# One expert's rows fetched by index instead of gathered by matrix products, and the index search moved from chunk 6 to chunk 2

## The chip, the cores and the metric

The kernel runs on 1 core of one Trainium2 chip. The metric is the device time of one execution in microseconds (us). TensorE is called PE here, VectorE DVE, ScalarE ACT, GpSimd POOL and SyncE SP. PE has two clock levels, 1.2 and 2.4 GHz, and the profile gives the granted share of the full one.

## What is computed

Three layers follow each other: attention with a top-32 mask, a soft mixture of 8 experts over 32 slots, and a noisy top-2 mixture of 8 experts. The change lies in the last one, whose reference is:

```python
def _moe2_ref(x, w_gate, w_noise, noise, w1, w2):      # N=2304 D=512 E=8 F=1024
    logits = x @ w_gate
    noise_scale = np.log1p(np.exp(x @ w_noise))
    noisy_logits = logits + noise_scale * noise
    top2 = np.argpartition(-noisy_logits, 2, axis=1)[:, :2]
    ...
    for e in range(E):
        for k in range(2):
            mask = top2[:, k] == e
            h = np.maximum(x[mask] @ w1[e], 0.0)
            out[mask] += top2_w[mask, k, None] * (h @ w2[e])
    return out
```

The second layer's output is a product of a [2304, 32] matrix of weights (`cn` in the kernel) and 32 slot outputs (`soT`). `top2_w` is the softmax over the two chosen logits. So the kernel never forms x in the third layer: a token is its row of 32 weights, and an expert's first layer is applied to the 32 slot outputs once (`soT` times w1[e], 32 x 1024) and then mixed per token.

## The kernel before

**Stages.** `attention` fills some 480 us of the span, `moe` computes the second layer, the gate and what the first expert needs, and `gated` runs the eight experts of the third layer from about 511 us on.

**An expert** takes up to CAP = 640 tokens in JT = 5 row groups of 128. `CTS[e]` (128 x 640) holds the 32 weights of each of its tokens in split form, transposed; `GSS[e]` holds `soT` times w1[e], split in a high and a low half (`gh`, `gl`) and stacked by `stacked_g` with four DMAs. Its hidden width of 1024 goes in 8 chunks of 128 columns; the loop variable n counts the 64 chunks of all experts, e = n // 8, c = n % 8. Chunk n consists of

- `split(n + 2)` (L1284): the weights w2[e] of a later chunk are split in `wh` (copy, on ACT for expert 0, else on DVE) and `wl` (DVE subtraction, L1292);
- `second(n, ...)` (L1294): 5 row groups of 3 products each (L1300 to L1302) into the accumulators `ACC`;
- `first(n + 2)` (L1268), between row groups 1 and 2: two products (L1276) into the PSUM tile `hp`, then `hh` = relu on ACT (L1281) and `hl` = the remainder on DVE (L1282). `hp` is one buffer, so `first(n + 3)` waits for `hl` of n + 2.

After chunk 7 `store(e)` (L1304) copies the accumulators and POOL adds them to the output rows of the expert's tokens by five indirect DMAs (L1312), whose row numbers `ids_of(e)` takes from the fetched rows.

**How an expert gets its tokens.** Experts 0 and 1 (ED = 2) have one-hot matrices: for each of 18 blocks of tokens `slot1` gives the place of each token, DVE or ACT builds a one-hot tile, and PE multiplies it with the weighted rows `xw`. For expert 0 that is `compact` (L1138), ahead of the chunks. For expert 1 it is `hot` (L1210) and `piece` (L1223), 34 products (L1229) in chunks 1, 2, 4 and 5 as the table `PIECES` says. At the pieces named in `WT1` the first layer of expert 2 (half a = 0) or 3 (a = 1) is computed beside them by `weigh1` (L936 to L940), two products side by side in PE's columns, and `pieces_end` (L1238) splits it into `gh`, `gl`.

Experts 2 to 7 are fetched: `addresses` (L1081, seven small DVE operations in chunk 0) computes the place of every (token, choice); `spread` (L1091) gives the steps that turn places into a list of rows: `far` (POOL) with `near` (ACT), or `same` (DVE), build one-hot tiles over the position, `columns` (two DVE and four POOL operations) one-hot tiles over the column, and `rows_of_slots` (L1122, chunk 6) multiplies them in 36 small products (L1125); five DVE operations make `ridx` of it. `rows(e)` (L1242) is five indirect DMAs of POOL that fetch the rows from `XD`, `slots(e)` (L1252) three DVE operations that split them, `turn` (L1261) five transposes by PE (L1264) and the copies to `CTS[e]`. In this version chunk 7 issues `rows(2)` and `rows(0)` (the latter for `ids_of(0)`), chunk 9 `rows(1)`; from then on `rows(e + 1)` is issued in chunk c = 1, `slots(e + 1)` follows in c = 3 and `turn` in c = 4 and 5.

**Order.** Each engine works through its own instructions in the order in which the code emits them; waits are by semaphore, and an instruction that waits holds back all behind it on its engine. SP issues the weight loads in the order of the list `order`; `MORE` (L174) says after which chunks one more load is issued, and a load waits until the buffer it overwrites has been read (`used`). First-layer weights of experts 4 to 7 are used by `first_weights` (L957) after chunks 18 and 19, four products side by side.

```python
1348                weighted(1, t2.tile([128, TT, NS], F32, name="xw", bufs=1), V)
1349                addresses()
1350                pairs, far, near, same, columns = spread(t2)
1351                for k in range(3):
1352                    far(k)
1353            if n in (1, 3, 6):
1354                near((1, 3, 6).index(n))
1355            if n == 3:
1356                columns()
1357                same(3)
1358                same(4)
```

Of the kernel before, what the change touches and what calls it, by code (L numbers as in the profile page):

```python
# [25 lines left out]
E, F, DM = 8, 1024, 512  # L26
NS = 32
NTOK = NB * S
TT = 18
CAP = 640  # L30
JT = CAP // 128
ROW = 36
ED = 2
ONACT = (2, 6, 10, 14)
NCH = 7
KW = S + 64
# [3 lines left out]
def moe_after_topk_attention(ctx: ExitStack, tc: tile.TileContext, q, k, v, phi, w1, w2, wg, wn, noise, u1, u2, qk, vt, out):  # L40
    nc = tc.nc
    V, A, G, T = nc.vector, nc.scalar, nc.gpsimd, nc.tensor

    def pool(name, bufs=1, stack=ctx, **kw):
        return stack.enter_context(tc.tile_pool(name=name, bufs=bufs, **kw))
# [55 lines left out]
    WT, wpool, held = {}, {"wa": wa}, {}  # L101
# [37 lines left out]
    def used(m, e):  # L139
        held.pop(slot[order.index((m, e))])  # L140
# [28 lines left out]


    H1, H2 = 4, 2

    PIECES = {1: 6, 2: 12, 4: 8, 5: 8}
    MORE = (0, 2, 4, 6, 8, 9, 14, 19, 22, 26, 30, 34, 38)  # L174
    FW, WT1, ENDS = (18, 19), (11, 13, 15, 17), (3, 6)

    def make_xtr(wk, xk, ps, soon, row, warm):

# [601 lines left out]
    def moe(st, xp, xs, fast):  # L780
# [9 lines left out]
        ps = pool("ps1", 1, st, space=PSUM)  # L790
# [277 lines left out]
        def place():  # L1068
            V.tensor_tensor(pe, po, cap8.unsqueeze(1).to_broadcast([128, TT, 8]), op=OP.add)
# [85 lines left out]
        def some(n):  # L1155
            for _, t in zip(range(n), todo):
                compact(t)
# [9 lines left out]
        some(H2)  # L1167
        A.copy(tots, tot[:, :144])
        place()
        some(8)  # L1170
        nc.sync.dma_start(XD[0:2 * NTOK].rearrange("(p r) f -> p (r f)", p=128), RW.rearrange("p c t f -> p (c t f)"))
        some(TT)
# [22 lines left out]
        def done():  # L1195
            tb_st.close()
            xs.close()
        gated(st, ps, halves, tw, gather, cts0, done, first_weights, weigh1, halve1, keep_g, stacked_g, GSS, begin, later,
              weighted, nt, slot1, xw, addresses, spread, rows_of_slots, ridx)


    def gated(st, ps, halves, tw, gather, cts0, done, first_weights, weigh1, halve1, keep_g, stacked_g, GSS, begin, later,
              weighted, nt, slot1, xw, addresses, spread, rows_of_slots, ridx):
        CTS, CX, XS, IDS, HH, HL, WH, WL, ACC = ({} for _ in range(9))

        H = CAP // 2
        part = []
        pieces = iter([(a, t) for a in range(2) for t in range(2 * a, TT)])

        def hot(a, t):  # L1210

            w = min(H, 128 * t + 128 - a * H)
            o = t2.tile([128, H], F32R, name="hot", bufs=6)[:, :w]
            n = nt[:, a * H:a * H + w]
            if t % 3:
                V.tensor_scalar(o, n, slot1[:, t, 1:2], None, op0=OP.is_equal)
            else:
                z = t2.tile([128, H], F32, name="far", bufs=1)[:, :w]
                A.activation(z, n, AF.Abs, bias=slot1[:, t, 1:2], scale=-1.0)
                A.activation(o, z, AF.Relu, bias=1.0, scale=-1.0)  # L1220
            return a, t, w, o

        def piece(a, t, w, o):  # L1223

            if t == 2 * a:
                part[:] = [ps.tile([128, 512], F32, name="tp")]
                if a == 0:
                    CTS[1] = t2.tile([128, CAP], F32R, name="cts")
            T.matmul(part[0][:64, :w], xw[1][:, t].rearrange("p l s -> p (l s)"), o, start=(t == 2 * a), stop=(t == TT - 1),  # L1229
                     skip_group_check=True)  # L1230

            if t in WT1:
                weigh1(2 + a, part[0], [WT1.index(t)])
            if t == TT - 1:
                for r, f in ((0, A.copy), (64, V.tensor_copy)):
                    f(CTS[1][r:r + 64, a * H:a * H + H], part[0][:64, :H])

        def pieces_end(a):  # L1238
            halve1(2 + a, part[0])
            used(2, 2 + a)  # L1240

        def rows(e):  # L1242
            xs = XS[e] = t2.tile([128, JT, ROW], F32, name="xs", bufs=3)
# [2 lines left out]
                    ap=ridx[:, e * JT + j:e * JT + j + 1], axis=0), bounds_check=2 * NTOK, oob_is_err=False)  # L1246

        def ids_of(e):
            ii = IDS[e] = t2.tile([128, JT], I32, name="ii")
            G.tensor_copy(ii, XS[e][:, :, NS])  # L1250

        def slots(e):  # L1252
# [15 lines left out]
        def first(n):  # L1268
            e, c = divmod(n, 8)

            p = [ps.tile([128, 512], F32, name=f"acc{i}") for i in ((1, 3), (2, 4))[n]] if n < 2 else halves()
            hh = HH[n] = tw.tile([128, CAP], F32R, name="hh")
            hl = HL[n] = tl.tile([128, CAP], F32R, name="hl")
            h = CAP // 2
            for a in range(2):
                T.matmul(p[a][:, :h] if n < 2 else p[:, a, :h], GSS[e][:, c * 128:c * 128 + 128],  # L1276
                         CTS[e][:, a * h:a * h + h], start=True, stop=True)
            for a in range(2) if n < 2 else [slice(None)]:
                x = p[a][:, :h] if n < 2 else p[:, :, :h]
# [14 lines left out]
        def second(n, js):  # L1294
            e, c = divmod(n, 8)
            for j in js:
                if c == 0:
                    ACC[j] = ps.tile([128, 512], F32, name=f"acc{(0, 1, 3, 2, 4)[j]}")
                r = slice(j * 128, j * 128 + 128)
                T.matmul(ACC[j], HH[n][:, r], WH[n], start=(c == 0), stop=False)  # L1300
                T.matmul(ACC[j], HH[n][:, r], WL[n], start=False, stop=False)  # L1301
                T.matmul(ACC[j], HL[n][:, r], WH[n], start=False, stop=(c == 7))  # L1302
# [18 lines left out]
        split(0, hi=False)  # L1321
        done()
        tl, t2 = pool("tl", 4, st), pool("t2", 2, st)
        first(0)
        split(1)
        first(1)
        for n in range(8 * E):
            e, c = divmod(n, 8)
            if (e, c) == (1, 0):
                later(t2)  # L1330
            m = n + 2
            some = [x for _, x in zip(range(PIECES.get(n, 0)), pieces)]
            some[:6] = [hot(*x) for x in some[:6]]
            if m < 8 * E:
                split(m)
            if n < 8 * E - 2:
                second(n, range(2))
                if m < 8 * E:
                    first(m)
                second(n, range(2, JT))  # L1340
            elif n == 8 * E - 1:

                for j in range(JT):
                    for i in (n - 1, n):
                        second(i, [j])
            if n == 0:
                begin()
                weighted(1, t2.tile([128, TT, NS], F32, name="xw", bufs=1), V)
                addresses()
                pairs, far, near, same, columns = spread(t2)  # L1350
                for k in range(3):
                    far(k)
            if n in (1, 3, 6):
                near((1, 3, 6).index(n))
            if n == 3:
                columns()
                same(3)
                same(4)
            if n in ENDS:
                pieces_end(ENDS.index(n))  # L1360
            for x in some[:6]:
                piece(*x)
            for x in some[6:]:
                piece(*hot(*x))
            if n == 6:
                rows_of_slots(ps.tile([128, 512], F32, name="tp"), pairs)
            if n == 7:
                keep_g(0)
                assert not list(pieces)
                rows(2)  # L1370
                rows(0)
                ids_of(0)
            if n == 9:
                rows(1)
                ids_of(1)
            if m % 8 == 7:
                used(3, m // 8)
            if e + 1 < E:
                if c == 1 and e + 1 != 4:
                    stacked_g(e + 1)  # L1380
                if c == 1 and e + 1 > ED:
                    rows(e + 1)
                if c == 3 and e + 1 >= ED:
                    slots(e + 1)
                if c == 4 and e + 1 >= ED:
                    turn(e + 1, 0, 4)
                if c == 5 and e + 1 >= ED:
                    turn(e + 1, 4, JT)
            if n in FW:
                first_weights(1, FW.index(n), ps.tile([128, 512], F32, name="tp"))  # L1390
            if n in MORE:
                more(32, 1)
            if (e, c) == (3, 1):
                stacked_g(4)
            if c == 6 and e >= ED:
                ids_of(e)
            if c == 7:
                store(e)

# [136 lines left out]
```

## Time and profile before

| what | value |
|---|---|
| median of 3 runs | 824.79 us (820.87 to 827.76) |
| the profiled execution's own time | 822.0 us |
| its span (first to last instruction) | 820.2 us |
| PE busy over the span | 768.7 us (94%) |
| DVE, ACT, POOL busy | 603.1, 500.3, 488.9 us |
| mean granted PE clock | 0.968 |

The profile comes from one execution, which is 2.8 us below the median. The page cuts the span in 40 slices of 20.5 us; its lines of the busy share (tenths) and of the granted clock are:

```profile
PE   8999999999999998999999978778999989999993
DVE  7999999999999998999982216963652645555540
ACT  5999999999999997999982115652231212222310
POOL 6888988889987886889660104230656235255233
PEclk9999999999999998999998989898999999999997
```

The experts of the third layer lie in slices 25 to 40. A busy PE is not a PE at its peak, and a line's "mean ns" of a matmul is its latency, longer than the step from one matmul to the next.

### The profile page before, as it was taken

The numbers are of one execution on the slowest core, as the hardware profiler recorded it, in microseconds if no ns is written. First come the engines' busy times: TensorE is split into PE (matmuls) and PEld (weight loads), VectorE is DVE, ScalarE is ACT, GpSimd is POOL, SyncE is SP. The second block draws the span as 40 slices with busy tenths as digits, with TensorE's granted clock in tenths as the row PEclk, the third lists the DMA queues.
The fourth block names the chain that finished last, engine by engine and source line by source line (L and its number), as shares of the span: only waits on it lengthen the run. The fifth ranks groups of instructions, "written<-read, shape, count | busy, mean of one in ns | idle before, by whom it ended". The sixth has DMA issues, their size and how long they took to land. (4 is left out here: it accounts for less than half of the span.)

```text
span 820.2 us, 17239 instructions
## 1 busy us (share of the span) xinstructions
PE 768.7 (94%) x5652; PEld 631.1 (77%) x5652; DVE 603.1 (74%) x2943; ACT 500.3 (61%) x1041; POOL 488.9 (60%) x477
## 2 busy tenths in 40 slices
PE   8999999999999998999999978778999989999993
PEld 4999999889998897989996333545885768778882
DVE  7999999999999998999982216963652645555540
ACT  5999999999999997999982115652231212222310
POOL 6888988889987886889660104230656235255233
PEclk9999999999999998999998989898999999999997
DMA  5486685754656546543755998821785987145044
GB/s 161 113 219 162 174 241 122 197 147 105 203 133 161 165 100 202 141 94 77 258 204 174 387 402 275 289 103 59 232 191 88 299 242 170 34 67 73 7 57 65
DMA packets 62085, 135.21 MB, mean 165 GB/s; under 512 B 12450, under 2 KB 13090, under 8 KB 61986
## 3 DMA queue, kind: packets, MB, share of 16 engines
q1 hardware_dynamic: 54946, 123.83, 50.0%
q0 software_dynamic: 7040, 10.18, 9.1%
q8 instruction: 46, 0.75, 0.4%
q14 instruction: 53, 0.43, 0.2%
HBM read 84.37 MB, written 17.97 MB: 125 GB/s over the span
## 5 line engine op out<-in xcount | busy, mean ns | idle before, releaser
L498 DVE MAX8 c<-s 128x8 f32<-128x82 f32 (+1 forms) x1008 | 224.2, 232 | 8.9 <-ACT s L480 4.8
L524 POOL TENSOR_TENSOR u<-g,s 128x576 f32<-128x576 bf16 x144 | 186.0, 1291 | 11.8 <-DVE c L498 5.7
L569 PE MATMUL av<-vb,et 128*128 128x65 f32 x1280 | 162.2, 270 | 0.0
L569 PEld LDWEIGHTS av<-vb,et 128*128 128x128 f32 x1280 | 159.0, 192 | 0.5 <-issue 0.4
L542 POOL TENSOR_SCALAR s<-s,mx 128x576 f32<-128x576 f32 x144 | 108.0, 750 | 54.3 <-ACT a L541 28.4
L1300 PE MATMUL acc<-wh,hh 128*128 128x512 f32 x320 | 129.4, 404 | 0.0
L1312 POOL DMA_INDIRECT out_dram<-y,ii x40 | 66.1, 1654 | 104.3 <-issue 70.3
L1302 PE MATMUL acc<-wh,hl 128*128 128x512 f32 x320 | 126.9, 396 | 0.0
L1281 ACT ACTIVATE hh<-hp 128x640 fp32r<-128x640 f32 x62 | 43.8, 706 | 136.1 <-PE hp L1276 115.1
L1301 PE MATMUL acc<-wl,hh 128*128 128x512 f32 x320 | 126.1, 394 | 0.0
L518 ACT ACTIVATE g<-s,PB 128x576 bf16<-128x576 f32 x144 | 112.6, 782 | 9.4 <-DVE PB L505 4.3
L547 PE MATMUL st<-identf,s 128*128 128x128 f32 x576 | 115.1, 280 | 2.0 <-POOL s L542 2.0
L462 PE MATMUL S<-ks,qs 128*128 128x288 f32 x600 | 114.4, 317 | 1.1 <-ACT s L480 1.1
L541 ACT ACTIVATE a<-s,TH 128x576 bf16<-128x576 f32 x144 | 114.9, 798 | 0.0
L535 DVE MAX8 TH<-u 128x8 f32<-128x585 f32 x144 | 109.7, 762 | 2.2 <-POOL u L524 2.1
L548 PE MATMUL st<-steep,a 128*128 128x128 bf16 x576 | 106.1, 220 | 0.0
L1282 DVE SCALAR_TENSOR_TENSOR hl<-hp,hh 128x640 fp32r<-128x640 f32 x62 | 51.1, 824 | 73.6 <-ACT hh L1281 65.0
L480 ACT COPY s<-S 128x576 f32<-128x576 f32 x141 | 91.4, 648 | 9.3 <-PE S L462 6.7
L547 PEld LDWEIGHTS st<-identf,s 128*128 128x128 f32 x576 | 84.9, 147 | 9.3 <-POOL s L542 2.9
L462 PEld LDWEIGHTS S<-ks,qs 128*128 128x128 f32 x600 | 84.9, 191 | 9.1 <-ACT et L554 2.5
L559 ACT ACTIVATE et<-st 128x512 f32<-128x512 f32 x144 | 85.7, 595 | 6.5 <-PE st L548 6.4
L501 DVE MAX8 mx<-c 128x8 f32<-128x56 f32 x432 | 87.2, 202 | 0.1
(348 smaller groups left out, 1297.5 us busy)
## 6 DMA issues: line engine op xcount, KB each, us to landing
wa<-in_moe_w_dram SPq DMA_DIRECT2D x11, 2048.0 KB
ks<-hl SPq DMA_DIRECT2D x60, 320.0 KB
wb<-in_moe_w_dram SPq DMA_DIRECT2D x5, 2048.0 KB
raw<-in_qk_dram SPq DMA_DIRECT2D x15, 608.0 KB
wy<-in_moe_w_dram SPq DMA_DIRECT2D x4, 2048.0 KB
wa<-in_moe_w_dram SPq DMA_DIRECT2D x16, 512.0 KB
wb<-in_moe_w_dram SPq DMA_DIRECT2D x16, 512.0 KB
vb<-in_vt_dram SPq DMA_DIRECT2D x16, 390.0 KB
```

The lines of the kernel that those rows point to most:

```text
L462: T.matmul(ph[hf][:, :288], QS[h][:, q0:q0 + 128], KS[h][:, l, ks], start=(n == 0), stop=(n == len(mm) - 1))
L498: V.max(C[i][:, c * 8:c * 8 + 8], SS[i][:, cut[c]:cut[c + 1]])
L518: A.activation(g, SS[i], AF.Sign, bias=PB[:, i:i + 1], scale=-UNDER, accum_out=SM[:, i:i + 1])
L524: G.tensor_tensor(u[:, 0:S], G1[i], SS[i], op=OP.mult)
L535: V.max(thr(i, 8), UU[i])
L541: A.activation(AP[i // 2][:, S * (i % 2):S * (i % 2) + S], SS[i], AF.Relu, bias=thr(i), scale=-1.0)
L542: G.tensor_scalar(SS[i], SS[i], -1.0, MX[i][:, 0:1], op0=OP.mult, op1=OP.add)
L547: T.matmul(o, SP[i // 2][:, ks], identf, start=True, stop=True, is_transpose=True)
L569: T.matmul(o, ET[i][:, c], VB[j % 2][:, h, c], start=(c == 0), stop=False, skip_group_check=True)
L1300: T.matmul(ACC[j], HH[n][:, r], WH[n], start=(c == 0), stop=False)
L1301: T.matmul(ACC[j], HH[n][:, r], WL[n], start=False, stop=False)
L1302: T.matmul(ACC[j], HL[n][:, r], WH[n], start=False, stop=(c == 7))
```

## The change

Expert 1 is fetched by index like experts 2 to 7 (ED = 1; `hot`, `piece`, `pieces_end`, `PIECES`, `WT1`, `ENDS` and the second `weighted` are gone). `addresses` is emitted ahead of expert 0's chunks, after `place` in the one-hot stage; `far`, `near` (two each instead of three), `columns` and `same` (three instead of two) all in chunk 0; `rows_of_slots` in chunk 2, between row groups 1 and 2; `rows(1)`, `rows(2)`, `rows(0)` at the end of chunk 2. The first layer of experts 2 and 3 is computed by the new `first_weights2` after chunk 3, four products side by side in place of two. `slots(1)` stands in chunk 4, `turn(1)` in chunk 5. From expert 1 on, `rows(e + 2)` is issued in chunk c = 5, that is four chunks and more ahead of where `rows(e + 1)` stood.

```diff
-ED = 2
+ED = 1
...
         some(H2)
         A.copy(tots, tot[:, :144])
         place()
+        addresses()
         some(8)
...
+        def first_weights2(p):
+            for c in range(4):
+                for r in range(4):
+                    e, n = 2 + r // 2, r % 2
+                    w = WT[2, e].rearrange("p (c f) -> p c f", c=4)
+                    T.matmul(p[32 * r:32 * r + 32], soT[:, c], w[:, c, n * 512:n * 512 + 512], start=(c == 0),
+                             stop=(c == 3), tile_position=(0, 32 * r))
+            for r in range(4):
+                e, n = 2 + r // 2, r % 2
+                rs, fs, o = slice(32 * e, 32 * e + 32), slice(n * 512, n * 512 + 512), slice(32 * r, 32 * r + 32)
+                A.copy(gh[0][rs, fs], p[o])
+                V.tensor_tensor(gl[0][rs, fs], p[o], gh[0][rs, fs], op=OP.subtract)
+            for e in (2, 3):
+                used(2, e)
...
             if n < 8 * E - 2:
                 second(n, range(2))
+                if n == 2:
+                    rows_of_slots(ps.tile([128, 512], F32, name="tp"), pairs)
                 if m < 8 * E:
                     first(m)
                 second(n, range(2, JT))
...
             if n == 0:
                 begin()
-                weighted(1, t2.tile([128, TT, NS], F32, name="xw", bufs=1), V)
-                addresses()
-                pairs, far, near, same, columns = spread(t2)
-                for k in range(3):
+                for k in range(2):
                     far(k)
+                    near(k)
+                columns()
+                for k in range(2, 5):
+                    same(k)
+            if n == 2:
+                rows(1)
+                rows(2)
+                rows(0)
+                ids_of(1)
             if n == 3:
+                first_weights2(ps.tile([128, 512], F32, name="tp"))
+            if n == 4:
+                slots(1)
+            if n == 5:
+                turn(1, 0, 4)
+                turn(1, 4, JT)
+                ids_of(2)
+                ids_of(0)
             if n == 7:
                 keep_g(0)
-                rows(2)
-                rows(0)
-                ids_of(0)
-            if n == 9:
-                rows(1)
-                ids_of(1)
+            if c == 5 and e and e + 2 < E:
+                rows(e + 2)
             if e + 1 < E:
-                if c == 1 and e + 1 > ED:
-                    rows(e + 1)
-                if c == 3 and e + 1 >= ED:
+                if c == 1 and e > 1:
+                    ids_of(e + 1)
+                if c == 3 and e:
                     slots(e + 1)
...
-            if c == 6 and e >= ED:
-                ids_of(e)
```

## Rows read from the trace of the kernel before

**Rows 1.** Timeline of PE, first products of two neighbouring chunks of expert 1.
```profile
583.20 0.46 PE L1276 MATMUL hp<-cts,gs 128*128 128x320 f32 x2
586.95 0.46 PE L1276 MATMUL hp<-cts,gs 128*128 128x320 f32 x2
```

**Rows 2.** Windows view; us, busy PE, PEld, DVE, ACT, POOL, clock, DMA, GB/s.
```profile
520.10:538.00 17.90, 13.45 (x52) 6.63 (x51) 12.68 (x22) 7.24 (x12) 5.92 (x3) 0.81 0.62 235
545.60:563.70 18.10, 13.64 (x51) 7.23 (x50) 9.17 (x18) 5.71 (x11) 3.52 (x3) 0.81 0.00 1
567.60:573.50 5.90, 2.51 (x38) 2.40 (x37) 1.39 (x2) 1.98 (x3) 0.00 (x0) 0.75 0.49 178
```

**Rows 3.** Waits of PE from 577.6 to 808 us: total, times, longest.
```profile
PE tp L1264 <- DVE cx L1258: 4.2, 3, 3.2
PE tp L1264 <- DVE gl L932: 2.0, 1, 2.0
```

**Rows 4.** Timeline of DVE: `slots(3)`; start, us, line, operation, [idle before].
```profile
635.52 0.26 DVE L1256 CAST cx<-xs 128x160 fp32r<-128x160 f32 x1 [8.31 <-DMA xs<-xd,ridx]
```

**Rows 5.** Timeline of DVE: `compact`, start of `weighted`, start of `addresses`.
```profile
504.98 0.55 DVE L1148 TENSOR_SCALAR wx<-nt,slot 128x640 fp32r<-128x640 f32 x1 [0.88 <-PE acc L1152]
...
517.90 0.76 DVE L1050 TENSOR_TENSOR xw<-LT,g 128x576 f32<-128x576 f32 x1
...
519.87 0.45 DVE L1083 TENSOR_TENSOR oh<-oh,pe 128x288 f32<-128x288 f32 x1
```

**Rows 6.** Timeline: `far` on POOL, a DVE subtraction beside it, one without.
```profile
521.82 5.92 POOL L1099 TENSOR_TENSOR y<-nt,pc 128x1024 bf16<-128x1024 f32 x3 [15.96 <-DVE hot L1216]
...
525.91 2.38 DVE L1292 TENSOR_TENSOR wl<-wa,wh 128x512 fp32r<-128x512 f32 x1
...
530.25 0.69 DVE L1292 TENSOR_TENSOR wl<-wa,wh 128x512 fp32r<-128x512 f32 x1
```

**Rows 7.** Timeline: the lookup's tiles; POOL first and last of four.
```profile
541.49 0.81 DVE L1113 TENSOR_TENSOR cx<-nt,pc 128x640 bf16<-128x640 f32 x1
...
543.13 2.89 DVE L1108 TENSOR_TENSOR y<-nt,pc 128x1024 bf16<-128x1024 f32 x2
...
542.45 1.88 POOL L1115 TENSOR_TENSOR cx<-cx,ctn 128x640 bf16<-128x640 bf16 x1 [14.71 <-DVE cx L1113]
...
548.21 1.03 POOL L1116 TENSOR_SCALAR rr<-rr,pn 128x800 bf16<-128x800 bf16 x1
...
523.90 1.06 ACT L1103 ACTIVATE y<-y 128x1024 bf16<-128x1024 bf16 x1 [4.35 <-POOL y L1099]
```

**Rows 8.** Windows view: the lookup's 36 products; a later wait of PE.
```profile
571.10:573.50 2.40, 2.40 (x37) 2.40 (x37) 0.00 (x0) 0.00 (x0) 0.00 (x0) 0.50 0.96 331
668.00:671.20 3.20, 0.04 (x2) 0.01 (x1) 1.00 (x4) 0.00 (x0) 0.00 (x0) 1.00 0.81 311
```

**Rows 9.** Timeline of PE, first products around one pass of `first_weights`.
```profile
617.61 0.46 PE L1276 MATMUL hp<-cts,gs 128*128 128x320 f32 x2
...
625.15 0.46 PE L1276 MATMUL hp<-cts,gs 128*128 128x320 f32 x2
```

**Rows 10.** Timeline of PE, first products around one `turn` of expert 7.
```profile
761.99 0.46 PE L1276 MATMUL hp<-cts,gs 128*128 128x320 f32 x2
...
766.52 0.46 PE L1276 MATMUL hp<-cts,gs 128*128 128x320 f32 x2
```

**Rows 11.** Timeline of SP: expert 3's w1 goes out; windows view, later.
```profile
519.14 0.54 SPq L130 DMA_DIRECT2D wb<-in_moe_w_dram  x1
...
531.80:538.00 6.20, 6.20 (x29) 1.82 (x27) 1.28 (x4) 1.50 (x3) 0.00 (x0) 1.00 0.00 0
```

**Rows 12.** Timeline of POOL: first, last of ten fetches; expert 3's last.
```profile
575.01 1.26 POOL L1245 DMA_INDIRECT xs<-xd,ridx  x1 [25.78 <-DVE ridx L1131]
...
587.58 1.00 POOL L1245 DMA_INDIRECT xs<-xd,ridx  x1 [0.30 <-issue]
...
631.58 1.00 POOL L1245 DMA_INDIRECT xs<-xd,ridx  x1 [0.30 <-issue]
```

More of the change, by code (lines that the diff above doesn't have):

```diff
@@ L171, in moe_after_topk_attention @@
     H1, H2 = 4, 2
-    PIECES = {1: 6, 2: 12, 4: 8, 5: 8}
     MORE = (0, 2, 4, 6, 8, 9, 14, 19, 22, 26, 30, 34, 38)
-    FW, WT1, ENDS = (18, 19), (11, 13, 15, 17), (3, 6)
+    FW = (18, 19)
     def make_xtr(wk, xk, ps, soon, row, warm):
@@ L1198, in moe @@
         gated(st, ps, halves, tw, gather, cts0, done, first_weights, weigh1, halve1, keep_g, stacked_g, GSS, begin, later,
-              weighted, nt, slot1, xw, addresses, spread, rows_of_slots, ridx)
+              addresses, spread, rows_of_slots, ridx, soT, gh, gl)
     def gated(st, ps, halves, tw, gather, cts0, done, first_weights, weigh1, halve1, keep_g, stacked_g, GSS, begin, later,
-              weighted, nt, slot1, xw, addresses, spread, rows_of_slots, ridx):
+              addresses, spread, rows_of_slots, ridx, soT, gh, gl):
@@ L1204, in gated @@
         CTS, CX, XS, IDS, HH, HL, WH, WL, ACC = ({} for _ in range(9))
         H = CAP // 2
[L1207 to L1236, printed above, removed]
@@ L1238, in pieces_end @@
-        def pieces_end(a):
-            halve1(2 + a, part[0])
-            used(2, 2 + a)
+        def first_weights2(p):
[12 more added lines that the diff above has]
+                used(2, e)
@@ L1248, in ids_of @@
         def ids_of(e):
-            ii = IDS[e] = t2.tile([128, JT], I32, name="ii")
+            ii = IDS[e] = t2.tile([128, JT], I32, name="ii", bufs=4)
             G.tensor_copy(ii, XS[e][:, :, NS])
@@ L1323, in gated @@
         tl, t2 = pool("tl", 4, st), pool("t2", 2, st)
+        pairs, far, near, same, columns = spread(t2)
         first(0)
@@ L1331, in gated @@
             m = n + 2
-            some = [x for _, x in zip(range(PIECES.get(n, 0)), pieces)]
-            some[:6] = [hot(*x) for x in some[:6]]
             if m < 8 * E:
@@ L1347, in gated @@
                 begin()
-                weighted(1, t2.tile([128, TT, NS], F32, name="xw", bufs=1), V)
-                addresses()
-                pairs, far, near, same, columns = spread(t2)
-                for k in range(3):
+                for k in range(2):
                     far(k)
-            if n in (1, 3, 6):
-                near((1, 3, 6).index(n))
-            if n == 3:
[L1356 to L1366, printed above, removed]
+                    near(k)
[7 more added lines that the diff above has]
+                ids_of(1)
+            if n == 3:
+                first_weights2(ps.tile([128, 512], F32, name="tp"))
[6 more added lines that the diff above has]
+                ids_of(0)
             if n == 7:
                 keep_g(0)
-                assert not list(pieces)
-                rows(2)
-                rows(0)
-                ids_of(0)
-            if n == 9:
-                rows(1)
-                ids_of(1)
+            if c == 5 and e and e + 2 < E:
+                rows(e + 2)
             if m % 8 == 7:
@@ L1380, in gated @@
                     stacked_g(e + 1)
-                if c == 1 and e + 1 > ED:
-                    rows(e + 1)
-                if c == 3 and e + 1 >= ED:
+                if c == 1 and e > 1:
+                    ids_of(e + 1)
+                if c == 3 and e:
                     slots(e + 1)
-                if c == 4 and e + 1 >= ED:
+                if c == 4 and e:
                     turn(e + 1, 0, 4)
-                if c == 5 and e + 1 >= ED:
+                if c == 5 and e:
                     turn(e + 1, 4, JT)
```

## The prediction

> **What bounds the kernel now.** I read the page's 40 slices first: the last sixteen hold the experts, and PE's digits, 9 in most of them, are 7 and 8 where expert 0 is worked on. Then the timeline of PE. From expert 1 on one chunk follows the other every 586.95 - 583.20 = 3.75 us [rows 1]; nothing but PE's own products sets this. Eight chunks want 30.0 us. Expert 0's eight take much longer: the windows view shows three stretches in which PE does other things or waits [rows 2]. The first (17.9 us) and the second (18.1) each hold one chunk of work (chunks 2 and 5) and otherwise expert 1's pieces, the first layers of experts 2 and 3 beside them, and waits for the one-hot tiles; the clock is at 0.81 in both. The third (5.9) holds no chunk, only a wait and the lookup's 36 products. So expert 0 carries (17.9 - 3.75) + (18.1 - 3.75) + 5.9 = 34.4 us beside its chunks. Last, the waits of PE after expert 0 [rows 3]: 4.2 + 2.0 = 6.2 us, all ahead of transposes; the timeline of DVE shows what is behind the longest kinds: DVE stood 8.31 us before expert 3's split because the fetched rows had not landed [rows 4]. Whatever leaves these two sums moves the end, since every later chunk follows at PE's pace and the last stores hang on the last chunk.
>
> **What is removed.** All 34.4 us go: the pieces, their one-hot tiles, the pairwise first layers, the lookup in chunk 6. What comes instead is counted now, in the order of the chunks.
>
> *Addresses ahead of expert 0.* Seven DVE operations, from 519.87 to where POOL starts on them at 521.82, under 2.0 us [rows 5, 6]. In the one-hot stage DVE waits for PE to free tiles, 0.88 us before the operation at 504.98 [rows 5] and about as much before the next ones; two such waits swallow the move. I take 0; without that cover it is 2.0.
>
> *`far` beside chunk 0.* Two POOL operations of 5.92 / 3 = 1.97 us [rows 6], as soon as the memory of the one-hot stage is free, so beside DVE's first subtractions. Such a subtraction took 2.38 us beside `far` and 0.69 alone [rows 6]. The first one is on PE's path (chunk 0's second product needs it): +1.7 us. Bounds: 0, if `far` runs before the chunks, and both operations in full, 3.9.
> The Trainium skill (GPSIMD Engine Reference, section Specifications) says that POOL shares its SBUF interfaces with VectorE, and that VectorE instructions in a two-port mode or with two SBUF inputs contend. By that the next subtraction would be hit as well, the step would be 3.4 instead of 1.7 and the whole gain 25.4 instead of 27.1; the two rows on the subtraction agree with the rule, and none shows two in a row.
>
> *The lookup's tiles.* DVE had nothing left of expert 1's split `begin` at 517.90 [rows 5]; now it goes straight to `columns`, at 517.9 + 1.7 = 519.6. From `cx` at 541.49 to the end of `same` at 543.13 + 2.89 = 546.02 it took 4.5 us for both column tiles and one and a half `same` [rows 7]; the change has one full `same` more, 2.89 / 1.5 = 1.9. So DVE is through at 526.0. POOL starts after `cx`, at 519.6 + 0.8 = 520.4, and its four operations took 548.21 + 1.03 - 542.45 = 6.8 [rows 7]: 527.2. ACT's four `near` (1.06 each, 4.2 together [rows 7]) run meanwhile and end first. PE ends chunk 1 at 520.1 [rows 2] + 1.7, and two of chunk 2's five row groups (1.4) later, at 523.2, it reaches the 36 products. It waits 4.0 us for POOL, does the 16 of the first column tile within that, and then the other 20: 36 took 2.40 at the low clock [rows 8], so 1.3. Together 5.3. Bounds: 2.4 (no wait) and 9, if DVE and POOL stretch each other's operations by half again. `first` of chunk 4, behind the 36, wants DVE's `hl` of chunk 3, which is queued behind `same`: 526.0 + 0.69 + 0.8, just in time; it is the part of the 9 most likely to come.
>
> *Clock after that wait.* The clock fell to 0.50 in the stretch of the 36 products, behind a wait of 3.5 us (third stretch less these products) [rows 2, 8], and stayed at 1.00 through one of 3.2 [rows 8]. In the first stretch a mean of 0.81 over 17.9 us is 0.19 x 2 x 17.9 = 6.8 us at half clock [rows 2], in which 3.4 us of work are lost. Bounds 0 and 3.4; I take 1.5.
> The Trainium skill (TensorE: Matmul & The Clock Gate, Part 1) says that the throttled level is the default and activity releases it, so that any wait like this would be followed by low clock: 3.4 instead of 1.5, and a whole gain of 25.2. The row with 1.00 through 3.2 us agrees only in part.
>
> *`first_weights2`.* Four products side by side: a chunk with one pass of `first_weights` took 625.15 - 617.61 = 7.54 [rows 9], so 3.8 for the pass. Its weights: expert 3's, wanted at about 536, went out at 519.14, and no DMA ran any more from 531.8 on [rows 11]; no wait. The split behind it (four operations each on ACT and DVE) fits beside chunk 4.
>
> *Fetching expert 1.* Five DVE operations give `ridx` near 530.5. Ten fetches started 575.01 to 587.58, 1.4 us apart [rows 12], so the first five are issued by 537; the last one of expert 3 started at 631.58 and the rows were there at 635.52 [rows 4, 12], 3.9 later. Landed by about 541. `slots(1)` comes up on DVE near 544. No wait, bounds 0 and 3.
>
> *`turn(1)`.* The later one cost 766.52 - 761.99 - 3.75 = 0.8 [rows 1, 10]; with its two halves back to back on one PSUM tile 1.2, bounds 0.8 and 2.
>
> Sum in expert 0: 1.7 + 5.3 + 1.5 + 3.8 + 1.2 = 13.5 in place of 34.4, so 20.9 us gained. At the upper bounds (2.0 + 3.9 + 9 + 3.4 + 3.8 + 3 + 2 = 27.1) 7.3 are left, at the lower (0 + 2.4 + 0 + 3.8 + 0.8 = 7.0) 27.4.
>
> **Later experts.** `rows(e + 2)` goes out in chunk 5 of expert e, some six chunks (22 us) ahead of its split instead of two, so the waits for fetched rows and what they delay go: 6.2 [rows 3]. The weight loads are tied to chunks and buffers as before and keep their distance from their use; if a load becomes what is late next, the gain shrinks to 0 at worst. I take 6.2.
>
> Total 20.9 + 6.2 = 27.1 us. The profiled execution took 822.0, so 794.9. It lies below the median of the runs by 824.79 / 822.0 = 1.0034, and so I forecast 797.6 us. About 1% (8 us) is what a measurement of this kernel tells from no change.
>
> **Rivals.**
> *A: the lookup becomes the bound of chunks 0 to 3.* DVE and POOL hold each other up, the wait is at its upper end and the clock falls. For it: the 2.38 against 0.69. Against it: POOL is busy for only 3.9 + 6.8 = 10.7 us in all. Terms at upper bounds for `far`, the wait and the clock (3.9 + 9 + 3.4 in place of 8.5): 7.8 more, 805.4.
> *B: the later waits don't go*, because weights are late in place of rows: 6.2 less, 803.8. For it: DMA share 0.81 beside a late fetch [rows 8]. Against: the rows alone were what DVE waited for.
> *C, slower:* the wait in chunk 2 drops the clock and it does not come back. Place: chunks 2 and on. Price: at half clock a chunk costs up to 3.75 more, so a little over seven chunks eat the 27 us and ten make it over 1% slower; through the end of expert 1 (14 chunks) it is 797.6 + 52 = 850. Against it: the three stretches held 6.8, 0.19 x 2 x 18.1 = 6.9 and 0.25 x 2 x 5.9 = 3.0 us of half clock [rows 2], never more, and whole chunks followed each time.
> *D: no change.* `slots(1)` stands at the head of DVE and rows land 27 us late, near 568, so that all gained is lost: 825. Against: even fifteen fetches one after the other with the last's 3.9 us end at 530.5 + 14 x 1.4 + 3.9 = 554.
>
> **Chances.** Forecast (within 793 to 803) 0.61, A 0.18, B 0.15, C 0.03, D 0.03. Faster by over 1%: forecast, A and B, 0.94; within 1%: 0.03; slower 0.03. The forecast's own range is 793 to 803; for 8 in 10 it runs from 789 (expert 0 near its lower bounds, 6 us less, and some of the scatter of the runs) to 810 (A and half of B).
>
> **What would show it.** Right: `first` of chunk 10 some 19 to 22 us earlier than before; PE waits once, 3 to 5 us, for POOL's last column tile ahead of the 36 products; eight rounds of `first_weights2` in 3.8; no wait of DVE for fetched rows from expert 1 on; PE's total wait after expert 0 under 1 us. Wrong: a wait of DVE at `slots(1)`; more than one stretch of low clock after chunk 2; waits for weights in experts 2 to 4; or the one-hot stage ending later than before.

## The result and the profile after

| | before | after |
|---|---|---|
| median of 4 runs each, us | 822.83 | 794.63 (792.42 to 799.87) |
| ratio, with its 95% interval | | 0.9658 [0.9587, 0.9729] |
| profiled execution, us | 822.0 | 792.9 |
| its span, us | 820.2 | 791.1 |
| mean granted clock | 0.968 | 0.979 |
| `first(0)`, start in the span | 511.49 | 509.35 |
| `first(0)` to `first(10)` | 67.96 | 49.44 |
| `first(10)` to the end of the span | 240.75 | 232.31 |

The forecast was 797.6 and 27.1 us of gain. The span is 29.1 shorter: 18.5 in expert 0 (predicted 20.9), 8.4 behind it (predicted 6.2), and 2.1 ahead of expert 0's chunks (`first(0)` starts earlier; in the other profiles of kernels with the same code up to there it starts between 507.8 and 517.8, so this part is scatter). 18.52 + 8.44 = 26.96 belong to the change.

The 40 slices of the page after, 791.1 / 40 = 19.8 us each; expert 0 lies in slices 26 to 28, with 8, 7 and 8 for PE, and the clock's digit falls to 8 in slice 27 alone:
```profile
PE   8999999999999999899999997878999999999993
PEclk9999999999999999899999998989999999999997
```
The windows view of after, over `first(0)` to `first(10)`, the step of chunk 2, and the one stretch of low clock (columns as in [rows 2]); they answer to [rows 2]:
```profile
509.35:558.79 49.44, 42.16 (x221) 31.11 (x222) 32.64 (x51) 20.76 (x34) 28.93 (x25) 0.93 0.79 266
...
516.86:527.39 10.53, 6.31 (x54) 5.33 (x53) 9.78 (x9) 4.15 (x6) 7.73 (x4) 0.79 0.88 312
...
522.80:529.60 6.80, 4.65 (x42) 4.24 (x42) 5.31 (x10) 1.21 (x2) 3.81 (x3) 0.51 1.03 419
```
Of the three stretches with a clock of 0.75 to 0.81 one is left. What PE waits for between 509 and 556 us, in the view of waits of after (total, times, longest):
```profile
PE tp L1123 <- DVE hl L1262: 2.1, 1, 2.1
PE tp L1123 <- POOL cx L1114: 2.1, 1, 2.1
PE hp L1256 <- DVE hl L1262: 1.7, 1, 1.7
PE acc L1256 <- ACT cts L1176: 0.8, 1, 0.8
PE tp L1244 <- ACT cts L1246: 0.7, 1, 0.7
PE acc L1281 <- DVE wl L1272: 0.5, 1, 0.5
```
From 556 us on the same view is empty: the 6.2 us of [rows 3] are gone to the last tenth. The first two lines are the lookup's waits, the third is one that the prediction did not have, the fourth stands ahead of `first(0)` as it did before, the fifth is `turn(1)`, the last is `far`'s effect on a subtraction. The first line names `hl`, which the lookup's products do not read: the last 20 begin 0.05 us after POOL's last column operation (526.05), just as the first 16 begin 0.05 after POOL's second (522.78), and `hl` ends in the same 0.05. In the timeline of PE the same places:
```profile
512.71 0.45 PE L1256 MATMUL hp<-cts,gs 128*128 128x320 f32 x2
516.86 0.45 PE L1256 MATMUL hp<-cts,gs 128*128 128x320 f32 x2
...
522.83 1.15 PE L1123 MATMUL tp<-cx,y 128*128 128x80 bf16 x16 [2.10 <-POOL cx L1114]
526.10 1.49 PE L1123 MATMUL tp<-rr,y 128*128 128x80 bf16 x20 [2.12 <-DVE hl L1262]
527.39 0.88 PE L1256 MATMUL hp<-cts,gs 128*128 128x320 f32 x2
...
545.44 0.56 PE L1256 MATMUL hp<-cts,gs 128*128 128x320 f32 x2 [1.75 <-DVE hl L1262]
```
The distance from one first product (L1256) to the next is a step; 3.74 is one without anything beside it. `first(0)` and `first(1)` start together, so nine steps lead to `first(10)`. They are 3.36, 4.15, 10.53, 4.95, 7.49, 5.61, 5.32, 3.74 and 4.29 (before: 2.56, 3.72, 11.44, 10.31, 3.72, 11.43, 10.52, 9.97, 4.29). The experiments below are read by these steps.

### The profile page after: what moved, and what is told of

It is laid out like the page before. It is cut to its first block, busy times and chain, and to the rows that moved or that the text cites. A ratio compares the mean times of both kernels' runs of the same rounds, so it can differ in the third digit from the quotient of the medians.

```text
span 791.1 us, 17130 instructions
## 1 busy us (share of the span) xinstructions
PE 751.4 (95%) x5623; PEld 624.7 (79%) x5623; DVE 592.2 (75%) x2919; ACT 488.2 (62%) x1017; POOL 487.4 (62%) x476
## 5 line engine op out<-in xcount | busy, mean ns | idle before, releaser
L1280 PE MATMUL acc<-wh,hh 128*128 128x512 f32 x320 | 127.2, 398 | 0.1
```

## The experiments

**Early fetch alone, in the kernel before.**
```diff
-                if c == 1 and e + 1 > ED:
-                    rows(e + 1)
+            if c == 5 and e and e + 2 < E:
+                rows(e + 2)
...
-            if c == 6 and e >= ED:
-                ids_of(e)
+                if c == 1 and e > 1:
+                    ids_of(e + 1)
```


> The kernel before the change, with only the early fetch: rows(e + 2) in chunk c = 5 of expert e, ids_of(e + 1) in c = 1. Theory (the early fetch alone carries the later gain): the steps around the first turn of experts 3 to 7 fall to 4.2, 7 us in sum, span about 813, ratio 0.991. Rival (it needs the shorter expert 0): steps and time as before, ratio 1.000.

Measured: 813.97 us (4 runs), ratio 0.9893 [0.9825, 0.9961]. The steps with a first `turn` of experts 3 to 7 fell from 6.44, 7.59, 5.07, 4.89 and 4.53 to 4.21 or 4.22 each, 7.5 us in sum. So the later experts' gain is the fetch's and does not need the shorter expert 0. From `first(10)` to the end the span is 7.0 us shorter here (815.2 - 581.4 = 233.8 against 240.75); one new wait of 0.9 for ACT in expert 2 is in it.

**Late fetch, in the kernel after.**
```diff
-            if c == 5 and e and e + 2 < E:
-                rows(e + 2)
...
-                    ids_of(e + 1)
+                    rows(e + 1)
...
+            if c == 6 and e > 2:
+                ids_of(e)
```


> The changed kernel, but rows(e + 1) issued in chunk c = 1 of expert e again for experts 3 to 7 (ids_of(e) in c = 6), as before the change. Theory (the 8 us gained after expert 0 come from fetching earlier): the steps around the first turn of experts 3 to 7, 4.20 us in the changed kernel, grow back to 6.4, 7.6, 5.1, 4.9 and 4.5 or near that, 7 us in sum; ratio to the kernel before about 0.975. Rival (those waits went because a shorter expert 0 loosened the traffic of weights and stores): the steps stay at 4.2 and the ratio at 0.966.

Measured: 799.23 us (5 runs), ratio 0.9719 [0.9652, 0.9786]. The five steps: 4.20, 6.37, 5.10, 5.52, 4.68, so 4.9 us over 4.20. The timeline of DVE, split of experts 3, 4 and 7:
```profile
612.37 0.25 DVE L1236 CAST cx<-xs 128x160 fp32r<-128x160 f32 x1
...
651.83 0.26 DVE L1236 CAST cx<-xs 128x160 fp32r<-128x160 f32 x1 [5.10 <-DMA xs<-xd,ridx]
...
746.01 0.26 DVE L1236 CAST cx<-xs 128x160 fp32r<-128x160 f32 x1 [3.42 <-DMA xs<-xd,ridx]
```
DVE waits for the rows again (3.84 and 4.27 before the splits of experts 5 and 6), except for expert 3, whose rows had landed: the mechanism holds, its size was 4.9 of the 7 expected.

**No tensor work on POOL.** `far` and `near` go, all five tiles are made by `same`, and DVE does POOL's four column operations:
```diff
-                    G.tensor_tensor(x[:, :, 0], ...
-                    G.tensor_scalar(x[:, :, 1], ...
+                    V.tensor_tensor(x[:, :, 0], ...
+                    V.tensor_scalar(x[:, :, 1], ...
...
-                for k in range(2):
-                    far(k)
-                    near(k)
...
-                for k in range(2, 5):
+                for k in range(5):
                     same(k)
```


> The changed kernel with no tensor work on POOL in the lookup: five `same` on DVE in place of two `far` and three `same`, and the four column operations of POOL on DVE too. Theory (a DVE operation with two SBUF inputs waits for the POOL operation beside it): the first two subtractions of chunk 0 take 0.7 each in place of 1.6, `same` on 1024 columns about 1.2 in place of 1.5, the first step falls from 3.36 to 2.6, the second from 4.15 to 3.75, and DVE ends the lookup's tiles at about the same time as now. Rival (these operations are just as long alone): 1.6 and 1.5 stay, and the lookup waits 3 us longer.

Measured: 805.33 us (1 run; its stage started 8 us later than after's). The first two steps are 2.57 and 3.71 again, 1.2 us less than in after; steps 3 and 4 are 11.43 and 5.59 in place of 10.53 and 4.95, since the lookup now waits for DVE's tiles, so that up to there nothing is gained. The rival's 3 us more of waiting did not come either. The timeline of DVE (the last line is one `same` of full size):
```profile
517.99 0.69 DVE L1272 TENSOR_TENSOR wl<-wa,wh 128x512 fp32r<-128x512 f32 x1
...
525.08 0.82 DVE L1113 TENSOR_TENSOR cx<-cx,ctn 128x640 bf16<-128x640 bf16 x1
...
528.70 1.22 DVE L1106 TENSOR_TENSOR y<-nt,pc 128x1024 bf16<-128x1024 f32 x1
```
Against it, after's own timelines of DVE and POOL:
```profile
508.78 1.90 POOL L1097 TENSOR_TENSOR y<-nt,pc 128x1024 bf16<-128x1024 f32 x1 [4.64 <-PE acc L1150]
...
510.64 2.34 POOL L1097 TENSOR_TENSOR y<-nt,pc 128x1024 bf16<-128x1024 f32 x1
...
509.60 1.62 DVE L1272 TENSOR_TENSOR wl<-wa,wh 128x512 fp32r<-128x512 f32 x1
...
511.95 1.59 DVE L1272 TENSOR_TENSOR wl<-wa,wh 128x512 fp32r<-128x512 f32 x1
...
518.77 2.29 DVE L1106 TENSOR_TENSOR y<-nt,pc 128x1024 bf16<-128x1024 f32 x1
...
523.24 2.01 DVE L1272 TENSOR_TENSOR wl<-wa,wh 128x512 fp32r<-128x512 f32 x1
...
518.09 1.89 POOL L1113 TENSOR_TENSOR cx<-cx,ctn 128x640 bf16<-128x640 bf16 x1 [5.10 <-DVE cx L1111]
520.09 2.69 POOL L1114 TENSOR_SCALAR cx<-cx,pn 128x640 bf16<-128x640 bf16 x1
522.75 1.96 POOL L1113 TENSOR_TENSOR rr<-rr,ctn 128x800 bf16<-128x800 bf16 x1
524.82 1.23 POOL L1114 TENSOR_SCALAR rr<-rr,pn 128x800 bf16<-128x800 bf16 x1
```
A subtraction takes 0.69 alone and 1.6 beside `far`; a `same` of full size 1.22 alone, and 2.29 where it starts beside POOL's multiplication. By these rows DVE's operation is not slowed by a factor: the subtractions end 0.55 us after the POOL operation that was running when they began (508.78 + 1.90 = 510.68 and 509.60 + 1.62 = 511.22; 512.98 and 513.54; 524.71 and 525.25), the `same` 1.08 after it (519.98 and 521.06), as if they had stood still until then. The 2.38 of [rows 6] ends 0.55 after `far` as well (its third operation ran from 525.77 to 527.74). So what such an operation loses depends on how much of POOL's is left when it starts. The other direction shows too: POOL's four operations last from 518.09 to 526.05, 8.0 us, where [rows 7] had 6.8.

**What ends the lookup's wait.** Two late things stand at the same time in chunk 2: POOL's last column operation (526.05) and DVE's `hl` of chunk 3 behind three `same` (526.10). It is not by chance that they end together: the subtraction ahead of `hl` (523.24, 2.01 us) was held by POOL's third operation. Three kernels move one or both.

Lookup and fetch one chunk later:
```diff
-                if n == 2:
+                if n == 3:
                     rows_of_slots(ps.tile([128, 512], F32, name="tp"), pairs)
...
-            if n == 2:
+            if n == 3:
                 rows(1)
```

> The changed kernel, with rows_of_slots and the fetches of rows 1, 2, 0 one chunk later (chunk 3). First theory (the 4.2 us that PE waits in chunk 2 are for POOL's column tiles alone, over at 526.05 in the changed kernel's profile): PE does the rest of chunk 2 meanwhile, and the steps from first to first that are 10.53 and 4.95 in the changed kernel become some 3.75 and 7.5, 4 us less in sum. Second theory (hl of chunk 3, queued on DVE behind the three `same`, is over at 526.10 and holds first of chunk 4 through the one PSUM tile hp just as long): the wait is only renamed, to 5.5 us before first of chunk 4; the two steps are about 9.3 and 6.2, nothing gained in sum.

The three `same` one chunk later:
```diff
+            if n == 1:
                 for k in range(2, 5):
                     same(k)
```


> The changed kernel, with the three `same` of DVE emitted after chunk 1's products, so behind hl of chunk 3 in place of ahead of it; the lookup stays in chunk 2. First theory (only POOL's column tiles are late): steps of 10.53 and 4.95 as in the changed kernel, since `same` still ends by 526. Second theory (two late things end together): the same 10.5 and 5, because now `same` and POOL hold the lookup until 526 while first of chunk 4 is free; only this together with the later lookup gains. A rival to both (hl of chunk 3 was the one late thing): 6.5 in place of 10.53.

Both:

> Both: the three `same` behind hl of chunk 3, and the lookup and its fetches in chunk 3. First theory: 4 us less than the changed kernel in the steps up to first of chunk 5, as by the later lookup alone. Second theory: the later lookup alone gains nothing and the two together 4 to 5 us: first of chunk 4 follows its forerunner by 4.5 to 5, the next step by 6 (36 products, at most 1 us of wait), 10.5 to 11 in sum in place of 15.5. slots(1) in chunk 4 may then wait up to 1 us for the fetched rows.

Measured, steps 3 and 4 (10.53 and 4.95 in after, 15.48 in sum): 9.29 + 6.58 = 15.87 with the lookup later, 9.57 + 5.39 = 14.96 with `same` later, 4.61 + 6.11 = 10.72 with both. PE's waits there, lookup later:
```profile
PE hp L1256 <- DVE hl L1262: 5.4, 1, 5.4
```
`same` later:
```profile
PE tp L1123 <- POOL rr L1114: 3.7, 1, 3.7
```
both (total of what is left), and the windows view of that kernel over the lookup (columns as in [rows 2]):
```profile
PE hp L1256 <- DVE hl L1262: 1.5, 2, 0.8
...
517.00:535.00 18.00, 16.45 (x119) 11.11 (x118) 11.70 (x17) 6.56 (x10) 11.65 (x9) 1.00 0.75 259
```
Each change alone leaves the other late thing, and so gains nearly nothing; together they give 4.8 us in these two steps. The clock is part of it: with both moved it stays at 1.00 through the lookup. But the times were 800.35, 798.5 and 795.61 (1 run each), because steps 6 and 7 grew: 5.82 and 13.26, 9.99 and 7.36, 6.12 and 11.58 in place of 5.61 and 5.32. That is taken up below.

**The wait ahead of `first(7)`.** The timeline of after, ACT and DVE, first and last of the four copies and subtractions behind `first_weights2`, and what is queued behind them:
```profile
538.51 0.57 ACT L1217 CAST gh<-tp 32x512 fp32r<-32x512 f32 x1 [4.98 <-PE tp L1212]
...
539.12 0.68 DVE L1218 TENSOR_TENSOR gl<-tp,gh 32x512 fp32r<-32x512 f32 x1 [4.72 <-ACT gh L1217]
...
543.11 0.70 DVE L1218 TENSOR_TENSOR gl<-tp,gh 32x512 fp32r<-32x512 f32 x1 [0.65 <-ACT gh L1217]
...
544.56 0.83 DVE L1262 SCALAR_TENSOR_TENSOR hl<-hp,hh 128x640 fp32r<-128x640 f32 x1
545.30 0.25 DVE L1236 CAST cx<-xs 128x160 fp32r<-128x160 f32 x1
```
Copy and subtraction take turns, 538.51 to 543.81, and `hl` of the next chunk comes only then. The copies and the subtractions moved behind `slots(1)`:
```diff
-                first_weights2(ps.tile([128, 512], F32, name="tp"))
+                p2 = ps.tile([128, 512], F32, name="tp")
+                first_weights2(p2)
...
                 slots(1)
+                halves2(p2)
```


> The changed kernel, with the split of first_weights2's result (four copies on ACT, four subtractions on DVE) emitted after chunk 4's products and after slots(1) in place of the end of chunk 3. Theory (PE's 1.75 us wait before first of chunk 7 is hl of chunk 6 queued on ACT and DVE behind that split, whose copies and subtractions take turns for 5.3 us): the step from first of chunk 6 to first of chunk 7 falls from 5.61 to 3.75, the one after it (5.32) grows by at most 0.5. Rival (the split only moves its wait: turn(1) needs the PSUM tile that the split empties): the next step grows by as much, to 7.2, and the end stays.

Measured: 795.7 us (1 run); steps 3.71 and 7.07 in place of 5.61 and 5.32, together 0.15 less. The wait went on to `turn(1)`, which needs the PSUM tile that the late subtractions still read; the view of waits of PE has it:
```profile
PE tp L1246 <- DVE gl L1222: 1.7, 1, 1.7
```
The rival is what happened.

**`first_weights2` two abreast in place of four.**
```diff
-            for c in range(4):
-                for r in range(4):
+            for r0, c in itertools.product((0, 2), range(4)):
+                for r in (r0, r0 + 1):
```


> The changed kernel, first_weights2 with two products side by side in place of four (first both of expert 2 for all four c, then both of expert 3). Theory (four side by side run at once and two leave half of PE's columns idle): the step from first of chunk 7 to first of chunk 8... of the loop's chunk 3 to chunk 4, 7.49 us in the changed kernel, grows by 8 rounds of 0.43 = 3.4 to 10.9. Rival (PE lets the groups of columns run ahead whatever the order of issue): it stays at 7.5.

Measured: 803.74 us (1 run, its stage 8.5 us later); the step is 9.24 in place of 7.49, so 5.5 for the pass instead of 3.75. In the timeline of PE the second pair starts before the first has ended:
```profile
543.73 2.34 PE L1212 MATMUL tp<-wa,soT 128*32 128x512 f32 x10
545.49 0.62 PE L1212 MATMUL tp<-wb,soT 128*32 128x512 f32 x2
...
546.80 2.31 PE L1212 MATMUL tp<-wb,soT 128*32 128x512 f32 x10
```
The result lies between the two expectations: four column groups side by side do pay, but pairs cost less than twice as much, as their groups overlap at the seam.

**Where steps 6 and 7 went.** Three kernels on one chip: after once more, both moves of the lookup once more, and these with the subtractions of `first_weights2` split over chunks 3 and 4 and `slots(1)` moved to chunk 5:
```diff
+            halves2(p, (0, 1))
...
+                halves2(p2, (2, 3))
...
-                slots(1)
```


> The changed kernel once more, for a comparison on one chip. In the last four profiles a wait of 3 to 8 us stood around chunks 4 to 6 of expert 0 that the changed kernel's profile did not have: PE's transposes ended, by their rows, 5 us before ACT's copy that waits for them began. Theory: this wait belongs to the execution (the chip and the profile taken on it), not to the order of the work; then the changed kernel may show it here too, its sixth to ninth steps of the first layer adding up to 3 to 8 us more than 5.61 + 5.32 + 3.74 + 4.29 = 18.96, and its times scatter as they did, 792 to 800. Rival: the wait comes from the order of those four; then the steps add up to 18.96 within 0.3 here, and the median is 793 to 797 as before.

> The lookup in chunk 3 with the three comparisons behind chunk 3's subtraction (e7_both) once more, timed in five rounds beside the changed kernel. Theory (the wait of 3 to 8 us belongs to the execution): the 4.8 us that its fourth and fifth steps gave (15.48 to 10.72) reach the end, and its median lies 4 to 5 us under the changed kernel's. Rival (the order itself brings the wait): the sixth to ninth steps are again some 7 us longer than the changed kernel's, and the medians differ by less than 1.5 us.

> As e7_again, and the subtraction of experts 2 and 3's first layer is split: two of its four pieces run behind their copies in chunk 3, the other two in chunk 4, and expert 1's split moves to chunk 5. The two pieces that leave chunk 3 take 2 x (0.58 + 0.69) = 2.5 us from what stands ahead of the subtraction that the next first layer waits for, so its wait of 1.87 goes. Theory (the wait of 3 to 8 us belongs to the execution): 4.8 + 1.9 = 6.7 us under the changed kernel's median, less up to 1.5 if expert 1's turn now waits for its split. Rival (the order brings it): it gains 1.9 at most beside the changed kernel, since PE catches up with the same late thing.

| | median of 6, us | ratio to before | steps 3, 4 | steps 6, 7 |
|---|---|---|---|---|
| before (11 runs) | 819.92 | | | |
| after | 802.69 | 0.9772 [0.9736, 0.9807] | 10.53, 5.47 | 9.84, 7.43 |
| both moved | 799.33 | 0.9755 [0.9721, 0.9790] | 4.60, 6.11 | 6.13, 13.19 |
| and split | 800.21 | 0.9770 [0.9730, 0.9809] | 4.61, 6.11 | 4.59, 13.12 |

Here `after` itself has the long steps, without any of the moves: they belong to the execution or to the chip, as the theory said. On this chip the change gains 17.2 us, not 28. Of the 4.8 and 6.7 us expected of the other two, 3.4 and 2.5 show in the median, with intervals that overlap after's, so that neither gain is clear of the scatter: the part of the theory that they would reach the end fell, as step 7 of the two is some 6 us longer than after's. The timeline of after in this second profile, PE's last product of `first_weights2`, ACT's copy of it, DVE's subtraction behind that:
```profile
541.68 0.60 PE L1212 MATMUL tp<-wa,soT 128*32 128x512 f32 x2
...
546.60 0.57 ACT L1217 CAST gh<-tp 32x512 fp32r<-32x512 f32 x1 [9.19 <-remote]
...
547.21 0.68 DVE L1218 TENSOR_TENSOR gl<-tp,gh 32x512 fp32r<-32x512 f32 x1 [8.94 <-issue]
```
In the first profile 0.1 us lay between product and copy (538.4 and 538.51), here 4.3 (542.3 and 546.60). PE went on with other products meanwhile and POOL kept issuing fetches; the trace holds no semaphore update of an engine from 538.2 to 545.0, and fewer records of landed transfers in all (5795 instead of 6177). What released the copy is named "remote", and the wait of DVE "issue": the views have no event to put there. So by these rows the signal was late, not the work. PE then waited for `first(7)`, and the granted clock fell once more:
```profile
553.54 0.90 PE L1256 MATMUL hp<-cts,gs 128*128 128x320 f32 x2 [5.97 <-issue]
...
551.40:558.20 6.80, 4.66 (x12) 3.69 (x13) 5.32 (x10) 2.31 (x4) 1.46 (x4) 0.50 1.01 357
```
Such a signal is 2.7 to 6.6 us late, at ACT's copy behind `first_weights2` or behind `turn(1)`, in all seven profiles from this chip and from the one of the three lookup kernels and the kernel without POOL work; they hold 5680 to 5795 records of landed transfers. The fetches were the suspect; the last kernel breaks up their string:
```diff
             if n == 2:
                 rows(1)
-                rows(2)
-                rows(0)
                 ids_of(1)
...
+            if n == 6:
+                rows(0)
+                ids_of(0)
...
+            if n == 8:
+                rows(2)
+                ids_of(2)
```


> In the changed kernel's second profile PE's product ended at 542.1 by its row, ACT's copy that waits for it began at 546.60, and between 538.2 and 545.0 no engine's semaphore update is recorded, while POOL issued the fetches of experts 1, 2 and 0 one behind the other. Here only expert 1's five fetches stand there; expert 0's move to chunk 6 and expert 2's to the chunk after expert 0's last. Theory (the updates are held up by the long string of fetches): the sixth and seventh steps of the first layer are 5.6 and 5.3 also in a profile with the landing records thinned out, 10.9 together in place of 17.3, and at most 2 to 3 us of it comes back where the other ten fetches now stand (chunks 6 to 9). Rival (the weight loads at full rate hold them up, or the 128x32 products): the two steps are 15 to 18 as in the second profile. If the records of this profile are complete (some 6180 landings, as in the changed kernel's first) the steps say nothing, and only the median does: 802.7 less 6 by the theory, 802.7 by the rival, on a chip of that kind.

Measured: 794.24 us (6 runs), before 822.73 in the same set, ratio 0.9669 [0.9630, 0.9708]; steps 6 and 7 are 5.61 and 5.30, with 5868 landing records. The timeline of PE and ACT:
```profile
537.66 0.60 PE L1212 MATMUL tp<-wa,soT 128*32 128x512 f32 x2
...
538.37 0.57 ACT L1217 CAST gh<-tp 32x512 fp32r<-32x512 f32 x1 [4.98 <-PE tp L1212]
```
The signal is on time in a profile whose records are thinned out, as the theory has it, and nothing came back in chunks 6 to 9 (steps 3.74 to 4.29). But it was another chip than that of the second profile, after itself was not run there, and the chip is a rival that this run does not exclude: with all fifteen fetches in a row the copy came 0.1 us behind its product in after's first profile, and again in those of the late fetch and of two abreast, which come from a chip that is neither of those two nor the last kernel's (6175 and 6178 records). Whether the shorter string or the chip put the signal on time stays open; after on the last kernel's chip would tell. Where the signals are on time this kernel is no faster than after's first 794.63.

## Why the prediction was right, step by step

The time fell at 794.63 in a range of 789 to 810; the profiled execution was forecast at 794.9 and took 792.9, of which 2.1 is the earlier start. The mechanism came as written, in expert 0 and behind it, but that the change's 26.96 us lie so near the 27.1 is in part luck: 2.4 too little in expert 0 and 2.2 too much behind it cancel. By the terms:

| term | predicted | after |
|---|---|---|
| removed from expert 0 | 34.4 | 67.96 less 2.56, 3.72, six of 3.74 and 4.29 = 35.0 |
| addresses | 0 | 0 (DVE's tiles still wait 0.41 for PE at 505.66) |
| `far` beside chunk 0 | 1.7 | 0.80 + 0.43 = 1.2 |
| lookup | 5.3 | 10.53 - 3.74 = 6.8 |
| clock after it | 1.5 | 4.95 - 3.74 = 1.2 |
| `first_weights2` | 3.8 | 7.49 - 3.74 = 3.75 |
| fetch of expert 1 | 0 | 0 (`slots(1)` at 545.30 without a wait) |
| split of `first_weights2` | 0 | 5.61 - 3.74 = 1.9 |
| `turn(1)` | 1.2 | 5.32 - 3.74 = 1.6 |
| gained in expert 0 | 20.9 | 35.0 - 16.5 = 18.5 |
| later experts | 6.2 | 8.4 |

*`far`.* Both subtractions beside it were lengthened, to 1.62 and 1.59. That is the case that the Trainium skill (GPSIMD Engine Reference, section Specifications) names, and the step that took only the first as hit was wrong about that. It came out smaller than either sum, 1.2 against 1.7 and 3.4, because each lost 0.9 instead of 1.7, and PE waited only 0.5 for the first. The 1.7 was what one subtraction lost that began 0.14 us behind the start of a `far`; here only 1.1 and 1.0 us of `far` were left.

*Addresses.* They are six operations, not seven, and took 2.9 us (501.40 to 504.33) where under 2.0 was counted; PE waits for no engine from 499.9 to the end of the one-hot stage (508.5), so they were covered.

*Lookup.* This term of the sum was too small by 1.5. PE reached the products at 520.73, did the first 16 between two waits of 2.10 and 2.12, as the prediction had it, and began the other 20 at 526.10: 5.4 us instead of 4.0. Those 20 took 1.29, as counted (1.3). The 1.4 is POOL's: its four operations lasted 8.0 in place of 6.8, which is the contention of rival A at a part of its price, and PE came 0.2 sooner after their start.

*Clock.* It fell once, behind the first of the two waits, and stayed at 0.51 for 6.8 us; the waits inside hid part of the loss. The Trainium skill (TensorE: Matmul & The Clock Gate, Part 1) says that the throttled level is the default and that activity releases it. In this profile low clock did follow the wait; but the 3.4 us that the prediction reckoned by that sentence were 1.2 in the step that follows. Rival C's price did not arise in this profile: there was no second stretch. With the late signal there was one, 6.8 us at 0.50 from 551.4 on.

*The failed step.* "The split behind it (four operations each on ACT and DVE) fits beside chunk 4" put this term at nothing, without a sum, and left out that the four pairs run in turn, 1.33 us apart, and that `hl` of the next chunk is queued behind the last on DVE. The cost is 1.9 us. The kernel that moved the split shows that it isn't free elsewhere either, as long as its PSUM tile is the one that `turn(1)` needs.

*Later experts.* The waits of [rows 3] were 6.2, the steps around the turns gave 7.5, here as in the kernel before with only the early fetch. In the kernel after with the late fetch they gave 4.9. The profile before, from which the 7.5 comes, has thinned-out records (5736), that of the late fetch has 6175; whether this makes the difference is not shown. The step of [rows 10], 4.53, which was taken as a turn that waits for nothing, is 4.20 now: 0.33 of it was the late fetch, and as much or more hung on the other turns that [rows 3] don't show. The remaining 0.9 is some fifty steps of 3.74 in place of 3.75 (0.5) and the end.

Rivals B and D are out by the empty view of waits and by `slots(1)`. What the prediction did not have at all is the late signal: with it the same change gains 17.2 us in place of the 27.1. That 802.69 still lies in the range says nothing for the mechanism; in that set of runs the kernel before is faster too, by 2.9 us (819.92 against 822.83).

## What to carry to other kernels

Where two late things end together, taking one away shows nothing; move both before a wait is called unavoidable. When a pass ends in a chain of copies and subtractions on two engines, count the chain, not the durations, and look at what stands behind its last link on each queue. Move a fetch by several chunks when its landing scatters: the early fetch was worth 4.9 to 7.5 us for no instruction at all. And compare two orders of work within one set of runs on one chip: the same kernel took 794.63 in one set and 802.69 in another.

## What was not expected of the hardware

DVE and POOL hold each other up. A subtraction of 128x512, 0.69 alone, took 1.6, 2.01 and 2.38 beside POOL, each time ending 0.55 after the POOL operation; a `same` took 2.29 in place of 1.22; POOL's scaling of 128x640 takes 2.69 with `same` beside it and 1.13 in the kernel with both moves.

On two chips a semaphore's signal came 2.7 to 6.6 us late while POOL issued fifteen fetches one behind the other, and the trace lost records; on another, and in after's first profile, it was on time with the same string. Why is open. Whether the signal is late also when nothing is recorded can't be told from these runs, since every time here comes from a recorded execution; the kernel before has thinned-out records as well (5736), the one with only the early fetch has not (6177).
